# Cosine attention and a hardswish layer: transfers of values by head on 128 partitions, casts in three pieces, biases as immediates

## The chip, the core and the metric

The kernel runs on one core of a Trainium2 chip. The metric is device time in microseconds (us) of one execution; lower is better. Besides TensorE (PE), VectorE (DVE), ScalarE (ACT) and GpSimd (POOL), the core has SyncE (SP), which here only issues DMA transfers, and 16 DMA engines that carry them out.

## What is computed

q, k and v have 8 batches, 12 heads, 448 tokens and 64 elements, in fp32. Attention is on normalised q and k, and its result goes through two matrix products with a hardswish between them (d_model 768, d_ff 2048, 3584 tokens):

```python
q_n = q / (norm(q) + 1e-06);  k_n = k / (norm(k) + 1e-06)
attn = softmax(q_n @ k_n.T / tau)            # tau = 0.1
x = (attn @ v) with the heads side by side   # 3584 x 768
h = x @ w_in
out = (h * clip(h + 3.0, 0.0, 6.0) / 6.0) @ w_out
```

## The kernel before, in words

**Work units.** A *pair* i (0 to 47) is two heads of one batch, A = head n and B = head n + 6, so that a batch is six pairs. Two pairs with neighbouring heads share their transfers: the load d = i // 2 of values brings heads n and n + 1 of group 0 (A) and group 1 (B).

**Tokens.** Token 7p + c of a head is row p (0 to 63) and piece c (0 to 6). Keys and values of one head stand on 128 partitions: rows with pieces 0 to 2 on partitions 0 to 63 and pieces 4 to 6 on partitions 64 to 127. That is three full 128-token groups. Piece 3 of A (partitions 0 to 63) and of B (64 to 127) make up a shared middle group, M.

**Loading values.** `load_v` (L200 to L209) issues four transfers on SP's queue, one for each group g and each half of the partitions: two heads on 64 partitions, four pieces of 64 elements each, 1,024 bytes in a row. One of three buffers of `big` takes them (`vr`, `NV` = 3); each head has five slots of 64 elements there. The lower half fills slots 1 to 4, the upper half slots 0 to 3. The slot that holds no values and yet is cast (4 above for A, 0 below for B) is set to zero once at the start (L968, L969).

**Casting values.** `vcast` (L280 to L288) turns the eight groups of a pair into bf16 in `vx` (four buffers), each with 65 columns, of which the last is 1 for the sum of the softmax. A single instruction on 128 partitions x 512 elements does it, on DVE (as a reduction over one element) for pairs 0 to 3 and on POOL for the others.

**Using values.** `values` (L457 and around) multiplies the exponentials by `vx` on PE into PV. For the middle group it takes all 128 rows for pairs below `FIRST` = 18, where the other head's half of `vx` must be zero; from pair 18 on it takes only the 64 rows that belong to the head.

**The order of work.** Every engine runs its instructions in the order in which they are written. Up to pair 17 that order is written out by hand in `PLAN`, with short names (`LQ` load q or k, `LV` load_v, `SQ` and `RE` squares and their sums, `NO` norms, `NM` normalise, `VC` vcast, `XD` transpose q and k by DMA, `CK`, `CS` and `CQ` copies of the transposed k and q, `SC` scores, `EX` exponentials, `VA` values, `FI` finish, `U` a unit of the layer). From pair 18 on, a loop writes one iteration for each pair; `VC` of pair i + 2 stands in iteration i, `XD` of the next two pairs in every even one, `LQ` of i + 7 in each and `LV` of load (i + 5) // 2 in every odd one. SP's queue holds the loads of q and k (L197), of values (L209), the transposes by DMA (L325, L509, L521) and most stores of the result (L603), all in that order. The weights come by POOL's queue. `busy_pv` (L923) and `busy` (L918) put matmuls on zeros in between at the start.

**Biases.** `norms` (L256) adds 1e-6 and `relu` in `mm1_unit` (L577) adds 0.5 through `bias=` from a tile of two columns, which two memsets fill (L972, L973). `relu` writes `u`, and DVE multiplies it into `gT` (L583).

Of the kernel before, what the change touches and what calls it, by code (L numbers as in the profile page):

```python
# [8 lines left out]
FP32 = mybir.dt.float32  # L9
BF16 = mybir.dt.bfloat16  # L10
AF = mybir.ActivationFunctionType
ALU = mybir.AluOpType
AX = mybir.AxisListType

EPS = 1e-6


FIRST = 18
# [43 lines left out]
def kernel(  # L62
# [10 lines left out]
    nc = tc.nc  # L73
    B, H, S, D = q.shape
# [3 lines left out]
    HP = H // 2  # L78
# [12 lines left out]
    const = ctx.enter_context(tc.tile_pool(name="const", bufs=1))  # L91
# [12 lines left out]
    KC = FCN // 2  # L104
# [13 lines left out]
    NV, NR = 3, 7  # L118


    RAW, VAL, SUM = 14 * D, 20 * D, KC * 128 // 2
    big = const.tile([128, (NR + 2) * RAW + NV * VAL], FP32, name="big", tag="big")

    def item(n):
        return big[:, n * RAW : (n + 1) * RAW].rearrange("p (g c d) -> p g c d", g=2, c=7)

    vr = [
        big[:, c : c + VAL].rearrange("p (i c d) -> p i c d", i=4, c=5)
        for c in range((NR + 2) * RAW, (NR + 2) * RAW + NV * VAL, VAL)
    ]  # L130
    NVX = 4
    vx = [const.tile([128, 8, D + 1], BF16, name=f"vx{i}", tag=f"vx{i}") for i in range(NVX)]
# [13 lines left out]
        [const.tile([128, 2, 14], FP32, name=f"{x}{i}", tag=f"{x}{i}") for x in ("ln", "nr", "le", "r")]  # L146
        for i in range(2)
    ]
    bias = const.tile([128, 2], FP32, name="bias", tag="bias")
    eps_bias, half_bias = bias[:, 0:1], bias[:, 1:2]  # L150
    ident = const.tile([128, 128], BF16, name="ident", tag="ident")

    PV = psum.tile([128, 2, 512], FP32, name="PV", tag="PV")
# [10 lines left out]
    engines = {"v": nc.vector, "p": nc.gpsimd, "a": nc.scalar, "s": nc.sync}  # L164
    issued = set()

    def needs(*what):
        for w in what:
            assert w in issued or any(x < 0 for x in w[1:] if isinstance(x, int)), w
# [31 lines left out]
    def load_v(d):  # L201
        needs(("VC", 2 * (d - NV)), ("VC", 2 * (d - NV) + 1))
        b, n = 2 * d // HP, 2 * d % HP
        for g in range(2):
            f = v[b, HP * g + n : HP * g + n + 2].rearrange("i (p c) d -> p i (c d)", c=7)
            t = vr[d % NV][:, 2 * g : 2 * g + 2, :, :].rearrange("p i c d -> p i (c d)")
            for half in range(2):
                o = t[64 * half : 64 * half + 64, :, (1 - half) * D : (5 - half) * D]
                nc.sync.dma_start(out=o, in_=f[:, :, 3 * half * D : (3 * half + 4) * D])  # L209

    def square(j, e, c0, n):

# [33 lines left out]
    def norms(d, *items):  # L246

        needs(("NM", 2 * d - 4), ("NM", 2 * d - 3))
        items = items or (0, 1)
        for x in items:  # L250
            needs(("RE", 2 * d + x))
        it = slice(items[0], items[-1] + 1)
        ln, nr, le, r = (t[:, it, :] for t in rs[d % 2])
        nc.scalar.activation(out=ln, in_=n2s[d % 2][:, it, :], func=AF.Ln)
        nc.scalar.activation(out=nr, in_=ln, func=AF.Exp, scale=0.5)
        nc.scalar.activation(out=le, in_=nr, func=AF.Ln, bias=eps_bias)  # L256
        nc.scalar.activation(out=r, in_=le, func=AF.Exp, scale=-1.0)  # L257
        for x in items:
            issued.add(("NO", d, x))
# [19 lines left out]

    def vcast(i, e):  # L280
        needs(("LV", i // 2), ("VA", i - NVX, 3))
        t = vr[i // 2 % NV][:, i % 2, 1:5, :]
        f = bass.AP(tensor=t.tensor, offset=t.offset, ap=[t.ap[0], [9 * D, 2], [D, 4], [1, D]])
        o = vx[i % NVX][:, :, 0:D].rearrange("p (g c) d -> p g c d", g=2)
        if e == "v":
            nc.vector.tensor_reduce(out=o, in_=f.rearrange("p g c (d x) -> p g c d x", x=1), axis=AX.X, op=ALU.max)
            return
        (engines[e].copy if e == "a" else engines[e].tensor_copy)(out=o, in_=f)  # L288

    z_of = {}  # L290
    unread = {}
# [1 line left out]
    def bank_of(name, reads):  # L293

        bank = {"Y": Y, "Z": Z}[name] if name else next_bank()
        key = id(bank)
        assert not unread.get(key), name
        unread[key] = reads
        return bank, key
# [231 lines left out]

    def tail(c, n):

        assert 2 * RAW <= c and c + n <= (NR + 2) * RAW + NV * VAL
        return big[:, c : c + n]

    TAIL = 2 * RAW
    g_last = tail(TAIL, FCN * (S + SR) // 2).bitcast(BF16).rearrange("p (f n) -> p f n", f=FCN)
    TAIL += FCN * (S + SR) // 2

    def g_of(b):
        if b == B - 1:
            needs(("NM", NP - 1), ("RE", NP - 1), ("VC", NP - 1))
            return g_last
        return gT[b % 2]
# [16 lines left out]
    def mm1_unit(b, fc):  # L562
        needs(*(("CX", i) for i in range(b * HP, (b + 1) * HP)))
        assert len(weights) <= 6 - 2 * (2 * fc // FCN)
        x, g, c0 = xT[b % 2], g_of(b), b % 2 * SR
        ps, key = bank_of(None, 1)
        for cc in range(CC):
            nc.tensor.matmul(  # L568
                ps[:, 0:S],
                w_in_sb[:, cc, fc * 128 : (fc + 1) * 128],  # L570
                x[:, cc, 0:S],
                start=(cc == 0),
                stop=(cc == CC - 1),
            )
        def relu():
            u = sb.tile([128, S], BF16, name="u", tag="u", bufs=3)
            nc.scalar.activation(  # L577
                out=u[:, :], in_=ps[:, 0:S], func=AF.Relu, bias=half_bias, scale=1.0 / 6.0
            )
            post["v"].append(lambda: product(u))  # L580

        def product(u):
            nc.vector.scalar_tensor_tensor(  # L583
                out=g[:, fc, c0 : c0 + S],
                in0=u[:, :],
                scalar=1.0,
                in1=ps[:, 0:S],
                op0=ALU.min,
                op1=ALU.mult,
            )  # L590
            unread[key] = 0
            g_done.add((b, fc))

        post["a"].append(relu)

    def result(b, t, cols, o, end=None):
# [39 lines left out]
    def firsts(b, *fcs):  # L636
        return [(mm1_unit, b, fc) for fc in fcs]

    def second(b):
# [12 lines left out]
    banks, parts, ready = {}, {}, set()  # L652
    late_sums = [
        {x: tail(c, SUM).bitcast(BF16).rearrange("p (c n) -> p c n", c=KC) for x, c in zip("167e", range(c, c + 4 * SUM, SUM))}
        for c in (TAIL, TAIL + 3 * SUM)
    ]
    late_sums[0].pop("e")
    TAIL += 7 * SUM
    wide = [big[:, c : c + MH] for c in range(0, 3 * MH, MH)]
    wide_late = [tail(c, MH) for c in range(TAIL, TAIL + 2 * (len(PAIRS) - LOOP) * MH, MH)]  # L660

    def sum_of(n, what):
# [211 lines left out]
    for b in range(2, B - 1):  # L874
        first = firsts(b, *range(FCN))
        for n, x in enumerate([0, 3, 3, 3, 3, 2]):
            i = (b + 1) * HP + n
            u = carry + [first.pop(0) for _ in range(x)]
            carry = []
            *p, last = products(TURNS[i])  # L880
            if i == NP - 1:
                p, last = [last], None
            x = 0 if n == 1 else 1 if n in (0, 5) and i > FIRST else 2
# [5 lines left out]
    b = B - 1  # L889
    f = firsts(b, *range(FCN))  # L890
# [50 lines left out]
    def whole_units(n, engines="av"):  # L941
# [5 lines left out]

    OPS = {
        "LQ": load_qk, "LV": load_v, "W": next_weights, "SQ": square, "RE": reduce, "NO": norms,
        "NM": normalise, "VC": vcast, "TR": transposes, "XD": crossbar, "XB": back_crossbar, "XP": back_two, "CQ": copy_q, "CK": copy_k, "CS": copy_k3, "SC": scores,  # L950
        "EX": exps, "VA": values, "FI": finish_values, "BK": back, "CX": copy_x, "U": unit, "UA": lambda: finish_units("a"), "UV": lambda: finish_units("v"),
        "GL": g_left, "WS": lambda x, *h: weight_sums(str(x), *((h[0] * KC // 2, KC // 2) if h else (0, KC))), "UU": whole_units, "D": busy, "DP": busy_pv, "OPEN": open_ring,
# [11 lines left out]
            do(op, *(int(a) if a.lstrip("-").isdigit() else a for a in args))  # L964


    for t in vr:
        nc.vector.memset(t[64:128, 0:2, 4, :], 0.0)  # L968
        nc.vector.memset(t[0:64, 2:4, 0, :], 0.0)  # L969
    zeros = xT[1][:, 0, :]  # L970
    nc.vector.memset(zeros, 0.0)
    nc.vector.memset(eps_bias, EPS)  # L972
    nc.vector.memset(half_bias, 0.5)  # L973
    make_identity(nc, ident)
    for t in vx:
        nc.vector.memset(t[:, :, D : D + 1], 1.0)
        nc.vector.memset(t[64:128, 3, D : D + 1], 0.0)
        nc.vector.memset(t[0:64, 4, D : D + 1], 0.0)
    for t in kz:
        nc.gpsimd.memset(t[:, :], 0.0)  # L980
    nc.gpsimd.memset(km[:, :, :], 0.0)
# [18 lines left out]
    for i in range(FIRST, NP):  # L1000
# [36 lines left out]
        n = 2  # L1037
# [59 lines left out]
```

## Time and profile before

| | |
|---|---|
| median of 3 runs | 405.61 us (405.17 to 407.64) |
| the profiled execution, its span | 405.6 us |
| busy: PE, DVE, ACT, POOL | 396.2, 288.9, 278.3, 233.5 us |
| granted clock of PE, mean | 0.998 |
| mean over DMA | 161 GB/s |
| values transfers to landing: shortest, median, longest | 2.6, 4.9, 11.1 us |

A span goes from the first to the last instruction of one execution. A line of a group names the line of the program, the engine, the operation, what is written and read, the shape and the count; then the busy time in us and the mean of one in ns; and last the idle time of the engine just before, with what ended it. A line of the stretches gives the stretch, its length, the busy time of each engine with the number of instructions, the granted clock of PE, the share of the 16 DMA engines' time in which they worked and the rate. A line of the queues gives packets, MB and the share of 16 engines; a line of the issues gives the count, the size of one and the median from issue to landing.

### The profile page before, as it was taken

The numbers are of one execution on the slowest core, as the hardware profiler recorded it, in microseconds if no ns is written. First come the engines' busy times: TensorE is split into PE (matmuls) and PEld (weight loads), VectorE is DVE, ScalarE is ACT, GpSimd is POOL, SyncE is SP. The second block draws the span as 40 slices with busy tenths as digits, with TensorE's granted clock in tenths as the row PEclk, the third lists the DMA queues.
The fourth block names the chain that finished last, engine by engine and source line by source line (L and its number), as shares of the span: only waits on it lengthen the run. The fifth ranks groups of instructions, "written<-read, shape, count | busy, mean of one in ns | idle before, by whom it ended". The sixth has DMA issues, their size and how long they took to land.

```text
span 405.6 us, 9619 instructions
## 1 busy us (share of the span) xinstructions
PE 396.2 (98%) x3696; PEld 234.5 (58%) x3696; DVE 288.9 (71%) x503; ACT 278.3 (69%) x609; POOL 233.5 (58%) x228
## 2 busy tenths in 40 slices
PE   7899999999989999999999999999999999999996
PEld 4666565555655555655555556556555556555554
DVE  5888777766998777777857887587656666645663
ACT  4899998888467687687767778778757755225230
POOL 6799645761483996587475874886674600410060
PEclk9999999999999999999999999999999999999999
DMA  8899989979988749886799649977964522140134
GB/s 286 251 251 244 236 237 226 184 112 192 223 208 190 184 109 199 200 220 143 172 196 223 132 129 180 184 194 144 188 158 86 112 45 58 40 87 20 24 75 99
DMA packets 91566, 65.32 MB, mean 161 GB/s; under 512 B 56064, under 2 KB 89984, under 8 KB 91520
## 3 DMA queue, kind: packets, MB, share of 16 engines
q1 hardware_dynamic: 87408, 58.02, 62.4%
q0 software_dynamic: 3712, 6.29, 9.0%
q8 instruction: 29, 0.48, 0.5%
q10 hardware_dynamic: 400, 0.39, 0.3%
q14 instruction: 17, 0.14, 0.1%
HBM read 47.19 MB, written 11.01 MB: 143 GB/s over the span
## 4 chain that ended last, share of the span: by engine, by line
PE 91%; DVE 3%; DMA 3%; POOL 1%; SPq 1%; issue 0%; DVEq 0%; POOLq 0%
PE M L568 24%; PE M L741 17%; PE PV L457 13%; PE Y L568 6%; PE M L417 6%; PE Z L568 5%; PE Y L741 4%; PE Z L741 3%; PE M L615 3%; DMA big<-in_q_dram 3%; PE M L821 2%; PE Z L417 2%; PE Z L821 1%; PE Y L417 1%; PE PV L923 1%; PE SC L417 1%
## 5 line engine op out<-in xcount | busy, mean ns | idle before, releaser
L435 ACT ACTIVATE at<-M 128x448 bf16<-128x448 f32 x200 | 99.8, 567 | 16.4 <-PE M L417 14.3
L568 PE MATMUL M<-xT,w_in_sb 128*128 128x448 bf16 x522 | 110.7, 352 | 0.0
L568 PEld LDWEIGHTS <-w_in_sb 128*128 128x128 bf16 x768 | 71.9, 98 | 62.4 <-issue 2.5
L269 POOL TENSOR_TENSOR nrm<-big,r 128x896 bf16<-128x896 f32 (+1 forms) x48 | 79.4, 1658 | 26.0 <-ACT r L257 19.2
L577 ACT ACTIVATE u<-M,bias 128x448 bf16<-128x448 f32 x87 | 57.0, 655 | 26.0 <-PE M L568 25.5
L583 DVE SCALAR_TENSOR_TENSOR gT<-u,M 128x448 bf16<-128x448 bf16 x76 | 46.8, 618 | 38.0 <-ACT u L577 37.3
L226 POOL TENSOR_TENSOR big<-big 128x896 f32<-128x896 f32 (+3 forms) x39 | 63.4, 1628 | 10.0 <-DVE rc L477 5.1
L457 PEld LDWEIGHTS <-at 128*128 128x128 bf16 (+1 forms) x1536 | 54.8, 97 | 24.0 <-issue 14.7
L457 PE MATMUL PV<-vx,at 128*128 128x65 bf16 (+1 forms) x1536 | 64.3, 194 | 0.2 <-DVE on L478 0.2
L238 DVE TENSOR_REDUCE n<-big 128x14 f32<-128x896 f32 (+1 forms) x50 | 51.9, 1041 | 6.2 <-ACT big L224 5.5
L374 POOL COPY km<-tT 64x128 bf16<-64x128 bf16 x34 | 12.7, 372 | 59.6 <-DMA tT<-nrm 44.1
L770 POOL TENSOR_TENSOR big<-big 128x384 f32<-128x384 f32 x11 | 11.8, 1071 | 54.7 <-ACT big L789 54.6
L741 PEld LDWEIGHTS <-gT 128*128 128x128 bf16 x288 | 27.8, 98 | 20.5 <-DVE gT L719 0.8
L741 PE MATMUL M<-w_out_sb,gT 128*128 128x384 bf16 x208 | 37.9, 326 | 0.3 <-DVE gT L719 0.3
L288 POOL CAST vx<-big 128x512 bf16<-128x512 f32 x44 | 33.5, 765 | 3.5 <-DMA big<-in_v_dram 2.4
L435 ACT ACTIVATE at<-Z 128x448 bf16<-128x448 f32 x49 | 27.7, 565 | 9.9 <-PE M L417 7.1
L478 DVE TENSOR_TENSOR on<-PV,rc 128x512 bf16<-128x512 f32 x48 | 33.2, 691 | 1.7
L417 PE MATMUL M<-tT,kz 64*128 64x448 bf16 (+1 forms) x175 | 31.9, 351 | 1.0 <-DVE o L628 1.0
L741 PEld LDWEIGHTS <-gs 128*128 128x128 bf16 x224 | 21.6, 98 | 14.5
L568 PE MATMUL Y<-xT,w_in_sb 128*128 128x448 bf16 x132 | 28.6, 353 | 0.0
L435 ACT ACTIVATE at<-Y 128x448 bf16<-128x448 f32 x45 | 25.7, 570 | 3.1 <-PE Z L417 2.9
L741 PE MATMUL M<-w_sum,gs 128*128 128x384 bf16 x144 | 26.3, 326 | 0.0
(133 smaller groups left out, 565.2 us busy)
## 6 DMA issues: line engine op xcount, KB each, us to landing
big<-in_v_dram SPq DMA_DIRECT2D x96, 128.0 KB, 4.9
big<-in_k_dram SPq DMA_DIRECT2D x24, 448.0 KB, 5.3
big<-in_q_dram SPq DMA_DIRECT2D x24, 448.0 KB, 4.3
out_dram<-o SPq DMA_DIRECT2D x107, 96.0 KB, 2.2
w_in_sb<-in_moe_w_in_dram POOLq DMA_DIRECT2D x4, 768.0 KB, 10.2
w_out_sb<-in_moe_w_out_dram POOLq DMA_DIRECT2D x4, 768.0 KB, 9.1
tT<-nrm SPq DMA_TRANSPOSE x34, 3.4
xT<-on SPq DMA_TRANSPOSE x25, 3.8
```

Of the source, the lines that this page charges most:

```text
L226: engines[e].tensor_tensor(out=o, in0=i, in1=i, op=ALU.mult)
L238: nc.vector.tensor_reduce(out=n2s[d % 2][:, j % 2, c], in_=sq[:, :, :, :].rearrange("p g c d -> p (g c) d")[:, c, :], axis=AX.X, op=ALU.add,)
L269: engines[e].tensor_tensor(out=nrm[:, :, g, :].rearrange("p c g d -> p g c d"), in0=raw_of[j][:, g, :, :], in1=rs[d % 2][3][:, j % 2, :] . ...
L288: (engines[e].copy if e == "a" else engines[e].tensor_copy)(out=o, in_=f)
L417: nc.tensor.matmul(o, ks, qt[rows], start=True, stop=True)
L435: nc.scalar.activation(out=o, in_=x, func=AF.Exp, scale=inv_tau)
L457: nc.tensor.matmul(pv_out(j, h), at[rows, n, q_cols(i // HP, j)], vt[rows, 3 + h if name == "M" else 5 * h + int(name[1]), :], start=(name ...
L478: nc.vector.tensor_tensor(out=on[:, :, :, :].rearrange("p j h d -> p h j d"), in0=pv4[:, :, :, 0:D], in1=rc[:, :, :].to_broadcast([128, 2, ...
L568: nc.tensor.matmul(ps[:, 0:S], w_in_sb[:, cc, fc * 128 : (fc + 1) * 128], x[:, cc, 0:S], start=(cc == 0), stop=(cc == CC - 1),)
L577: nc.scalar.activation(out=u[:, :], in_=ps[:, 0:S], func=AF.Relu, bias=half_bias, scale=1.0 / 6.0)
L583: nc.vector.scalar_tensor_tensor(out=g[:, fc, c0 : c0 + S], in0=u[:, :], scalar=1.0, in1=ps[:, 0:S], op0=ALU.min, op1=ALU.mult,)
L741: nc.tensor.matmul(m, lhs[:, c, :], rhs[:, c, c0 : c0 + width], start=(base is None and c == 0), stop=(c == KC - 1), skip_group_check=True,)
```

## The change

- `load_v` issues four transfers again, each with one head on 128 partitions, four pieces (1,024 bytes) in a row. The source pattern has a count of 2 for the halves of the partitions, outermost, put ahead of the 64 rows. Group 0 takes pieces 0 to 3 and 4 to 7, group 1 pieces -1 to 2 and 3 to 6; piece 7 and piece -1 are those of the neighbouring row.
- The buffers have four slots a head in place of five. `big` keeps its size.
- The slot that was zero now holds those neighbours' values. For pairs 0 to 17 `vcast` therefore casts in three pieces: 128 x 384, 64 x 64 and 64 x 64. From pair 18 on it is one piece of 128 x 512, with the neighbours' values in the halves that `values` does not read.
- The zeros of `vx` are set over 65 columns in place of one; the memsets of `vr` go.
- The biases 1e-6 and 0.5 are immediates; their tile and its two memsets go.

```diff
-    RAW, VAL, SUM = 14 * D, 20 * D, KC * 128 // 2
-    big = const.tile([128, (NR + 2) * RAW + NV * VAL], FP32, name="big", tag="big")
+    RAW, VAL, SUM = 14 * D, 16 * D, KC * 128 // 2
+    BIG = (NR + 2) * RAW + NV * 20 * D
+    big = const.tile([128, BIG], FP32, name="big", tag="big")
...
-        for g in range(2):
-            f = v[b, HP * g + n : HP * g + n + 2].rearrange("i (p c) d -> p i (c d)", c=7)
-            t = vr[d % NV][:, 2 * g : 2 * g + 2, :, :].rearrange("p i c d -> p i (c d)")
-            for half in range(2):
-                o = t[64 * half : 64 * half + 64, :, (1 - half) * D : (5 - half) * D]
-                nc.sync.dma_start(out=o, in_=f[:, :, 3 * half * D : (3 * half + 4) * D])
+        for h in range(4):
+            f = v[b, HP * (h // 2) + n + h % 2].rearrange("(p c) d -> p (c d)", c=7)[:, 0 : 4 * D]
+            f = bass.AP(tensor=f.tensor, offset=f.offset - h // 2 * D, ap=[[4 * D, 2]] + list(f.ap))
+            o = vr[d % NV][:, h, :, :].rearrange("p c d -> p (c d)")
+            nc.sync.dma_start(out=o, in_=f)
...
-        nc.scalar.activation(out=le, in_=nr, func=AF.Ln, bias=eps_bias)
+        nc.scalar.activation(out=le, in_=nr, func=AF.Ln, bias=EPS)
...
-        t = vr[i // 2 % NV][:, i % 2, 1:5, :]
-        f = bass.AP(tensor=t.tensor, offset=t.offset, ap=[t.ap[0], [9 * D, 2], [D, 4], [1, D]])
-        o = vx[i % NVX][:, :, 0:D].rearrange("p (g c) d -> p g c d", g=2)
-        if e == "v":
-            nc.vector.tensor_reduce(out=o, in_=f.rearrange("p g c (d x) -> p g c d x", x=1), axis=AX.X, op=ALU.max)
-            return
-        (engines[e].copy if e == "a" else engines[e].tensor_copy)(out=o, in_=f)
+        t, o = vr[i // 2 % NV], vx[i % NVX]
+
+        def part(p, x, n, w):
+            s, c = 2 * (x // 4) + i % 2, x % 4
+            f = t[p, s : s + 1, c, :]
+            f = bass.AP(tensor=f.tensor, offset=f.offset, ap=[f.ap[0], [(12 - n) * D, w], [D, n], [1, D]])
+            y = o[p, x : x + 1, 0:D]
+            y = bass.AP(tensor=y.tensor, offset=y.offset, ap=[y.ap[0], [(8 - n) * (D + 1), w], [D + 1, n], [1, D]])
+            return f, y
+
+        if i < FIRST:
+            parts = [part(slice(0, 128), 0, 3, 2), part(slice(0, 64), 3, 1, 1), part(slice(64, 128), 4, 1, 1)]
+        else:
+            parts = [part(slice(0, 128), 0, 4, 2)]
+        for f, y in parts:
+            if e == "v":
+                nc.vector.tensor_reduce(out=y, in_=f.rearrange("p g c (d x) -> p g c d x", x=1), axis=AX.X, op=ALU.max)
+            else:
+                (engines[e].copy if e == "a" else engines[e].tensor_copy)(out=y, in_=f)
...
-                out=u[:, :], in_=ps[:, 0:S], func=AF.Relu, bias=half_bias, scale=1.0 / 6.0
+                out=u[:, :], in_=ps[:, 0:S], func=AF.Relu, bias=0.5, scale=1.0 / 6.0
...
-    for t in vr:
-        nc.vector.memset(t[64:128, 0:2, 4, :], 0.0)
-        nc.vector.memset(t[0:64, 2:4, 0, :], 0.0)
...
-    nc.vector.memset(eps_bias, EPS)
-    nc.vector.memset(half_bias, 0.5)
...
-        nc.vector.memset(t[64:128, 3, D : D + 1], 0.0)
-        nc.vector.memset(t[0:64, 4, D : D + 1], 0.0)
+        nc.vector.memset(t[64:128, 3, :], 0.0)
+        nc.vector.memset(t[0:64, 4, :], 0.0)
```

## The prediction

> **What bounds the kernel now.** I read the page first: busy time, queues, the chain, the DMA issues.
>
> ```profile
> span 405.6 us, 9619 instructions
> ...
> PE 396.2 (98%) x3696; PEld 234.5 (58%) x3696; DVE 288.9 (71%) x503; ACT 278.3 (69%) x609; POOL 233.5 (58%) x228
> ...
> q1 hardware_dynamic: 87408, 58.02, 62.4%
> q0 software_dynamic: 3712, 6.29, 9.0%
> ...
> PE 91%; DVE 3%; DMA 3%; POOL 1%; SPq 1%; issue 0%; DVEq 0%; POOLq 0%
> ...
> big<-in_v_dram SPq DMA_DIRECT2D x96, 128.0 KB, 4.9
> big<-in_k_dram SPq DMA_DIRECT2D x24, 448.0 KB, 5.3
> ```
>
> PE is busy 98% of the span and is 91% of the chain, so an edit on another engine gains little. Only 9.4 us of the span are without PE. The second thing to see is the DMA load: 62.4 + 9.0 = 71.4% of 16 engines, or 290 us on each engine if it is spread evenly. That is second only to PE and holds only while it is spread.
>
> Then I read the stretches, cut at the issue of the last values transfers (301.3 us) and at the last values cast (323.9 us):
>
> ```profile
> core 0: us, PE busy (x) PEld busy (x) DVE busy (x) ACT busy (x) POOL busy (x), PEclk, DMA share, GB/s
> 5.00:10.00 5.00, 5.00 (x23) 2.65 (x22) 2.82 (x6) 2.68 (x8) 2.66 (x3) 1.00 1.04 373
> 0.00:301.30 301.30, 295.82 (x2939) 175.73 (x2940) 230.03 (x407) 232.18 (x517) 208.24 (x202) 1.00 0.87 193
> 301.30:323.90 22.60, 22.60 (x217) 13.22 (x215) 13.32 (x23) 16.20 (x37) 11.22 (x15) 1.00 0.53 112
> 323.90:405.60 81.70, 77.81 (x544) 45.55 (x542) 45.58 (x74) 29.96 (x57) 14.09 (x13) 0.99 0.25 56
> ```
>
> While values are being loaded the 16 engines are 87% busy, so none of them has room for much more. The first line gives the rate of one engine under load: 373 GB/s over 16 engines at a share of 1.04 is 22.4 GB/s, or 45.7 ns for 1,024 bytes.
>
> The timeline of SP's queue shows the pace of the values loads (start, time for four issues):
>
> ```profile
> 208.94 2.66 SPq L209 DMA_DIRECT2D big<-in_v_dram  x4
> ...
> 299.26 2.66 SPq L209 DMA_DIRECT2D big<-in_v_dram  x4
> ```
>
> There are seven loads from the first to the second line, so a load comes every (299.26 - 208.94)/6 = 15.05 us. Last, the groups with shapes kept apart, for the edits on the engines:
>
> ```profile
> L577 ACT ACTIVATE u<-M,bias 128x448 bf16<-128x448 f32 x87 | 57.0, 655 | 26.0 <-PE M L568 25.5
> L435 ACT ACTIVATE at<-M 128x448 bf16<-128x448 f32 x200 | 99.8, 567 | 16.4 <-PE M L417 14.3 <-PE Y L417 1.7
> L288 POOL CAST vx<-big 128x512 bf16<-128x512 f32 x44 | 33.5, 765 | 3.5 <-DMA big<-in_v_dram 2.4 <-PE Z L314 1.0
> L286 DVE TENSOR_REDUCE vx<-big 128x512 bf16<-128x512 f32 x4 | 2.6, 675 | 0.0
> L374 POOL COPY km<-tT 64x128 bf16<-64x128 bf16 x34 | 12.7, 372 | 59.6 <-DMA tT<-nrm 44.1 <-PE M L417 13.1 <-PE Z L417 1.4
> L336 DVE COPY kz<-Z 64x64 bf16<-64x64 bf16 x16 | 3.0, 186 | 0.1
> ```
>
> **The edits on the engines.** *Biases:* 87 + 22 + 19 = 128 of `u` at 655, 649 and 654 ns, where the exponential of the same shape takes 567: 128 x 0.088 = 11.3 us less on ACT. 25 of `le` at 318 against 243 for `ln`: 1.9 us less. ACT waited 25.5 us for PE just before `u`, so this lengthens a wait. On the path lie only the three `le` of the start: 0.2 us. I take 0; the ends are -0.2 and, if every `u` were waited for, a gain capped by PE's 9.4 us.
>
> *Casts of pairs 0 to 17:* 14 are on POOL, 4 on DVE. A three-quarter piece costs between 3/4 of the whole and the whole: 0.46 to 0.61 us on POOL (median of L288 612 ns), 0.51 to 0.67 on DVE. A 64x64 piece on POOL lies between the 205 ns memset of 128x128 and the 372 ns copy of 64x128, on DVE at the 186 ns copy. So POOL pays 0.87 to 1.36 us for 0.61, about 0.5 more, 7 us in all; DVE 0.88 to 1.04 for 0.67, about 0.25 more, 1.0 in all. Three DVE casts stand at 17.8 to 19.9 us ahead of a copy that PE needs: 0.7 us on the path. POOL is full from 20 to 40 us, where 3 of its casts stand, so up to 1.5 us there; later it idles over a quarter of the time, which hides the rest. Sum of the casts: 0.7, ends 0 and 7.7 (all of POOL's and the three on DVE).
>
> *Memsets:* six of 0.17 us and two of 0.06 go; eight of one column (0.06 us) grow to 65 columns, at most 0.17 each as 64x128 fp32 does. DVE saves 0.2 to 1.1 us before its first data at 4.21 us, for which it had waited 0.72 us: 0. Without that cover it would be a gain of that size.
>
> *Issues on SP:* still 96, at 0.607 us the median. At the 0.46 us of a first q or k issue SP would save 14 us; SP mostly waits for results (38.2 us for DVE at L603), so 0. The cast of a pair now needs two of the four transfers, and a transfer waits for two casts fewer: both earlier or equal, 0.
>
> **The transfer itself decides.** Bytes (131,072), rows (128 of 1,024 bytes) and count are as before; the source pattern is not. Before, both sides began with 64 partitions. Now the destination begins with 128 partitions and the source with a count of 2 (the halves, 4 x 64 elements apart), then 64, then 256 elements. No row shows a transfer whose pattern begins with a count under 64, so I bound its cost from both sides. One end is that it spreads as before: 0. Before, it did spread: the fastest landed in 2.6 us, 50 GB/s with its latency, above two engines' 44.8. The other end is that it is cut along its outermost count, which leaves two shares on two engines:
>
> - Values on each of the two: 96 x 64 = 6,144 rows x 45.7 ns = 281 us. By the mean of q1 (62.4% x 16 x 405.6 us over 58.02 MB = 71.5 ns for 1,024 bytes) 439 us.
> - All else before the last values issue: 0.87 x 301.3 = 262 us on each engine, less the values' old part there, 768 x 71.5 ns = 55: 207 us. If all of its bytes went at 22.4 GB/s: (58.02 + 6.29 - 12.58) MB/16/22.4 = 144 us, 90% of it before 301.3: 130.
> - The start, 3.8 us, and the stretch from the last cast to the end, 81.7 us.
>
> The sum is 3.8 + 281 + 130 + 81.7 = 497 to 3.8 + 281 + 207 + 81.7 = 574; with 439 for the values 732. I take 45.7 ns, from the stretch of back-to-back loads, since it is the row nearest to a queue of 1,024-byte rows. Between 497 and 574 I take 555, nearer the upper: most of the other packets are small (56,064 under 512 bytes) and do not move at 22.4 GB/s. The check by the pace: one load is 256 x 45.7 ns = 11.7 us on each of the two engines, the rest of 15.05 us at the share of 0.87 is 13.1 - 2.3 = 10.8 (2.3 being 32 rows at 71.5), 22.5 in all, 7.4 over the pace; 20 to 24 loads of that are 148 to 178 us: 554 to 583. The engines' edits hide behind this: casts wait for values, and PE waits for casts.
>
> SP's queue and the two engines are shared: behind four values issues stand the transposes of q and k, the q and k loads and the result stores. They land late by up to 11.7 us, and kz (DVE), km (POOL) and the scores (PE) wait for them; that is how the delay reaches PE beside the values themselves.
>
> I choose two engines because the count of 2 is the only dimension along which the source can be cut into whole blocks in the order of its rows. That it was cut this way no row shows. The Trainium skill, "DMA: Bandwidth & Descriptors", section "Why a DMA increments its semaphore by 16 and not by 1", says that the number of engines is the largest up to 16 that divides the slowest dimension above 1 of both sides: of 128 and 2 that is 2. Its table gives some 27 GiB/s for an engine, by which the values would take an estimated 217 us in place of 281, and the sum would be 491. The same page's "Rules for kernel authors" speak for one 128-partition transfer in place of two on partition halves; by that the sum would be that of the first rival.
>
> **Rivals.**
>
> 1. *The transfer spreads over 16 engines.* Then only the edits on the engines count: 405.6 + 0.7 - 0.2 = 406.1. For it: bytes and rows are the same, and the destination counts 128. Against: the outermost count of the source.
> 2. *It spreads, and the three-piece casts reach the path.* POOL, full from 20 to 40 us, delays the normalised q and k that PE transposes: 405.6 + 7.7 = 413.3 at most. It decides over 1% once 4.1 us of it reach PE; against it, POOL idles 42% of the span.
> 3. *It spreads and lands sooner: faster.* The place is the start, where SP waited 4.6 us for k, 4.2 for q and 1.7 for values to land before it issued values. If landings fell from 4.9 to the shortest, 2.6, 47% of these 10.5 us would go, and all behind them would come 4.9 us earlier: 400.7. It decides from 4.1 us on. Against it: 8.8 of the 10.5 us are for q and k, which do not change.
> 4. *Two engines, but hidden by loads three ahead.* 281 + 130 us do not fit into 297 us: no chance.
>
> **The numbers.** Two engines 0.82: 555, own range 480 to 700 (0.97 of it; below 497 if waits overlap better, up towards 732 if packets on two engines run at the mean price). Rival 1 0.11, rival 2 0.04, rival 3 0.03. So 480 to 700 holds 0.82 x 0.97 = 0.80. About 1% is what a measurement of this kernel can tell from no change: faster 0.03, same 0.11, slower 0.86. The sum stands on the profiled execution, whose span is 405.6 us; the median of the runs is 405.61.
>
> **What would show it.** Right: the landing of `big<-in_v_dram` from 4.9 us to 12 or more; PE at some 70%, with casts waiting for values and km and kz for transposes; mean GB/s from 161 to 118. The page named above says that each engine used ends its share with an increment of its own; by that the packets would fall by 96 x 14 from 91,566 to 90,222. Wrong: a landing under 6 us with PE still at 98%; then rivals 1 to 3 are told apart by POOL's wait for casts and the landing in the first 30 us. The engines' steps: `u` at 567 ns, three casts on POOL at some 1.1 us together, SP's issue at 0.46 to 0.61.

## The result and the profile after

| | before | after |
|---|---|---|
| median of the runs | 405.72 us (4 runs) | 573.88 us (4 runs, 572.06 to 577.35) |
| ratio | | 1.414, 95% interval 1.408 to 1.421 |
| profiled execution, span | 405.6 us | 570.3 us |
| granted clock of PE, mean | 0.998 | 0.874 |

The change makes the kernel 168 us slower. The page of the changed kernel, in the lines that answer to those shown of before:

```profile
span 570.3 us, 9656 instructions
...
PE 430.8 (76%) x3696; PEld 246.1 (43%) x3696; DVE 285.6 (50%) x503; ACT 268.9 (47%) x609; POOL 233.4 (41%) x256
...
DMA packets 90222, 65.32 MB, mean 115 GB/s; under 512 B 54720, under 2 KB 88640, under 8 KB 90176
...
q1 hardware_dynamic: 86064, 58.02, 51.5%
...
PE 49%; DMA 23%; SPq 18%; DVE 5%; ACT 2%; issue 2%; POOL 1%; POOLq 0%; DVEq 0%
PE M L578 13%; SPq L207 13%; PE M L751 9%; DMA xT<-on 8%; PE PV L467 7%; DMA big<-in_v_dram 6%; DMA tT<-nrm 5%; DMA big<-in_k_dram 4%; PE Y L578 4%; PE Z L578 3%; PE M L427 3%; PE Y L751 3%; SPq L335 2%; SPq L196 2%; PE Z L751 2%
```

No engine is busy for more than 76%, and the mean over the 16 DMA engines has fallen, not risen: 51.5% of their time on this queue, after 62.4%. Yet DMA and the queue of SP are now 41% of the chain, and the issues of values alone (L207) are 13%, as much as the largest group of matmuls. A mean over 16 engines hides a queue in front of two. The bytes are the same (65.32 MB), and the packets are 1,344 fewer, 14 for each of the 96 values transfers. This is the count that the prediction gave for two engines in place of 16.

The packet records of the trace show the two engines more directly. They name no engine, but a packet of 1,024 bytes is always a row of values, so one can count how many of them are under way at once. In the changed kernel it is exactly two for 78% of the time in which any is under way, and never more than four; before, it was up to 23. All in all, values are under way for 282 us, where it had been 88.

The waits name what came late:

```profile
POOL km L384 <- DMA tT<-nrm: 132.2, 14, 14.8
...
POOL vx L298 <- DMA big<-in_v_dram: 66.5, 10, 12.8
...
PE M L578 <- DMA xT<-on: 38.0, 6, 8.3
...
DVE kz L374 <- DMA tT<-nrm: 34.2, 8, 7.6
```

The casts of values wait, but the transposes, which the change does not touch, are waited for longer. They stand behind the values in SP's queue. That queue shows how they are held up. These are the first values load of the start and most of one turn of the loop:

```profile
3.89 9.19 SPq L207 DMA_DIRECT2D big<-in_v_dram  x4
...
310.43 5.80 SPq L207 DMA_DIRECT2D big<-in_v_dram  x4
316.33 5.24 SPq L531 DMA_TRANSPOSE xT<-on  x1
321.67 3.69 SPq L335 DMA_TRANSPOSE tT<-nrm  x2
325.45 1.19 SPq L613 DMA_DIRECT2D out_dram<-o  x2
326.69 0.58 SPq L196 DMA_DIRECT2D big<-in_q_dram  x1
327.38 1.20 SPq L519 DMA_TRANSPOSE xT<-on  x1
```

The four issues of the first load took 3.38 us before and take 9.19 now; those in the loop mostly took 2.66 and take 5.8 to 7.0. The transpose of `xT` behind them took 1.3 and takes 5.24. The second column is the time for which SP was held by the issue. When it is held can be read in this turn: the first two of the four issues still take 0.60 and 0.55 us, the next two 1.88 and 2.63. The 512 rows of the load are under way from 313.0 to 323.9 us, and from 325.4 us on the issues of stores and loads take about 0.6 us each, as they did before the change. So SP is held while the two engines still have rows of values to move. The view of line L207 sums it up:

```profile
L207 SPq DMA_DIRECT2D big<-in_v_dram x96: 544/2582/11174, 3.9 to 459.9; - x96
```

The median issue is 2.58 us, where it was 0.61. Two engines need 64 x 45.7 ns = 2.9 us for the rows of one transfer. Added up to the last values issue, SP's issues come to 199 us of 302 before and to 426 us of 462 after: SP now issues 92% of that time.

### The profile page after: what moved, and what is told of

It is laid out like the page before. It is cut to its first block, busy times and chain, and to the rows that moved or that the text cites. A ratio compares the mean times of both kernels' runs of the same rounds, so it can differ in the third digit from the quotient of the medians.

```text
span 570.3 us, 9656 instructions
## 1 busy us (share of the span) xinstructions
PE 430.8 (76%) x3696; PEld 246.1 (43%) x3696; DVE 285.6 (50%) x503; ACT 268.9 (47%) x609; POOL 233.4 (41%) x256
## 2 busy tenths in 40 slices
DMA packets 90222, 65.32 MB, mean 115 GB/s; under 512 B 54720, under 2 KB 88640, under 8 KB 90176
## 3 DMA queue, kind: packets, MB, share of 16 engines
q1 hardware_dynamic: 86064, 58.02, 51.5%
## 4 chain that ended last, share of the span: by engine, by line
PE 49%; DMA 23%; SPq 18%; DVE 5%; ACT 2%; issue 2%; POOL 1%; POOLq 0%; DVEq 0%
PE M L578 13%; SPq L207 13%; PE M L751 9%; DMA xT<-on 8%; PE PV L467 7%; DMA big<-in_v_dram 6%; DMA tT<-nrm 5%; DMA big<-in_k_dram 4%; PE Y L578 4%; PE Z L578 3%; PE M L427 3%; PE Y L751 3%; SPq L335 2%; SPq L196 2%; PE Z L751 2%
## 5 line engine op out<-in xcount | busy, mean ns | idle before, releaser
L578 PE MATMUL M<-xT,w_in_sb 128*128 128x448 bf16 x522 | 125.2, 384 | 50.8 <-DMA xT<-on 38.0
L578 PEld LDWEIGHTS <-w_in_sb 128*128 128x128 bf16 x768 | 76.4, 104 | 126.0 <-issue 73.8
L587 ACT ACTIVATE u<-M 128x448 bf16<-128x448 f32 x87 | 48.7, 559 | 92.2 <-PE M L578 90.2
L467 PE MATMUL PV<-vx,at 128*128 128x65 bf16 (+1 forms) x1536 | 69.6, 200 | 18.8 <-POOL vx L298 15.1
L467 PEld LDWEIGHTS <-at 128*128 128x128 bf16 (+1 forms) x1536 | 59.6, 101 | 48.4 <-issue 37.0
L384 POOL COPY km<-tT 64x128 bf16<-64x128 bf16 x34 | 9.9, 290 | 137.3 <-DMA tT<-nrm 132.2
L298 POOL CAST vx<-big 128x512 bf16<-128x512 f32 (+2 forms) x72 | 33.5, 476 | 77.2 <-DMA big<-in_v_dram 66.5
L427 PE MATMUL M<-tT,kz 64*128 64x448 bf16 (+1 forms) x175 | 36.6, 392 | 23.5 <-DMA tT<-nrm 23.0
L427 PEld LDWEIGHTS <-kz 64*128 64x128 bf16 (+1 forms) x296 | 14.3, 97 | 74.4 <-DVE kz L374 32.5
L578 PE MATMUL Y<-xT,w_in_sb 128*128 128x448 bf16 x132 | 32.0, 384 | 0.0
L222 ACT ACTIVATE big<-big 128x896 f32<-128x896 f32 (+4 forms) x12 | 9.0, 768 | 44.4 <-DMA big<-in_k_dram 39.8
```

What stands on the lines that cost most here:

```text
L427: nc.tensor.matmul(o, ks, qt[rows], start=True, stop=True)
L467: nc.tensor.matmul(pv_out(j, h), at[rows, n, q_cols(i // HP, j)], vt[rows, 3 + h if name == "M" else 5 * h + int(name[1]), :], start=(name ...
L578: nc.tensor.matmul(ps[:, 0:S], w_in_sb[:, cc, fc * 128 : (fc + 1) * 128], x[:, cc, 0:S], start=(cc == 0), stop=(cc == CC - 1),)
L587: nc.scalar.activation(out=u[:, :], in_=ps[:, 0:S], func=AF.Relu, bias=0.5, scale=1.0 / 6.0)
```

## The experiments

In each, the time is the median, and the ratio to the kernel before comes from runs on the same chip.

**Only the outermost count: 128, 4, 8.** Everything of the change stays except the source pattern.

```diff
-            f = bass.AP(tensor=f.tensor, offset=f.offset - h // 2 * D, ap=[[4 * D, 2]] + list(f.ap))
+            f = bass.AP(tensor=f.tensor, offset=f.offset - h // 2 * D, ap=[[7 * D // 2, 128], [1, 4 * D]])
```

> The changed kernel with one thing different: the source of a values transfer is one count of 128 rows (a row every 3.5 pieces) in place of 2 x 64. Bytes, rows of 1,024 bytes, destination on 128 partitions, number of transfers, casts and biases stay; the rows hold other values than the reference needs, so only its time counts. Theory A (the transfer is cut along its outermost count, so the changed kernel uses two engines): the time goes back to 406.1 us, within 400 to 413, and the landing of values is under 8 us. Theory B (128 partitions as destination, or reading neighbours' rows, makes the transfer slow): it stays at 560 to 580. Theory C (three-piece casts hold POOL up): it stays at 560 to 580.

Measured: 405.61 us, ratio 1.001 (0.998 to 1.004). Theory B (the 128 partitions or the neighbours' rows make the transfer slow) and theory C (the casts do) fall. The page of this kernel has the packets of before again, and a landing:

```profile
DMA packets 91566, 65.32 MB, mean 161 GB/s; under 512 B 56064, under 2 KB 89984, under 8 KB 91520
...
big<-in_v_dram SPq DMA_DIRECT2D x96, 128.0 KB, 4.0
```

```diff
+            f = bass.AP(tensor=f.tensor, offset=f.offset - h // 2 * D, ap=[[75 * D, 4], [7 * D, 32], [1, 4 * D]])
```

> The changed kernel with the source of a values transfer as 4 x 32 rows in place of 2 x 64; same bytes, rows, destination and count; the rows overlap and hold other values than the reference needs, so only its time counts. Theory A: four engines take 3,072 rows of 45.7 ns each, 140 us in place of 281; with 207 us of other transfers that is 347 us of the 301 us before the last values issue, so the DMA still binds a little: 421 us, within 408 to 440. Theories B and C: 560 to 580.

Measured: 460.81 us, ratio 1.135 (1.130 to 1.141).

```diff
+            f = bass.AP(tensor=f.tensor, offset=f.offset - h // 2 * D, ap=[[48 * D, 8], [7 * D, 16], [1, 4 * D]])
```

> The same with 8 x 16 rows; the values are again not those of the reference. Theory A: eight engines take 1,536 rows each, 70 us; with 207 us of other transfers that is 277 of 301 us, so PE binds again: 406 to 412 us. Theories B and C: 560 to 580.

Measured: 418.73 us, ratio 1.030 (1.026 to 1.034). The time follows the outermost count: 573.9, 460.8, 418.7 and 405.6 us for 2, 4, 8 and 128. The packets follow too. First the page with 4, then the page and the chain with 8:

```profile
DMA packets 90414, 65.32 MB, mean 143 GB/s; under 512 B 54912, under 2 KB 88832, under 8 KB 90368
```

```profile
DMA packets 90799, 65.32 MB, mean 157 GB/s; under 512 B 55297, under 2 KB 89217, under 8 KB 90753
...
PE 68%; DMA 18%; POOL 6%; DVE 3%; issue 2%; SPq 1%; ACT 1%; POOLq 0%
```

That is 1,152 = 96 x 12 fewer than before with 4, and 767, one off 96 x 8, with 8. The rows under way at once say the same: with 4 the most frequent number is 4, with 8 it is 8, and with 128 there are 16 or more for 23% of the time. The theory of the outermost count stands, but both times lie above the ranges that it gave, by 21 us and by 7. The expectation had only set the work on each engine against the time there is. With 4, SP's issues of values come to 106 us, where they are 47 with 128, and the longest single one is 6.4 us, so the queue is held here too. With 8 they come to 66 us and SP is 1% of the chain, so its queue does not set the pace there; transfers are 18% of it, and those of values 11%.

**The rest of the change with the transfers of before.** Four slots, casts in pieces and immediates stay; each transfer takes two heads on 64 partitions.

```diff
-        for h in range(4):
...
+        for g in range(2):
+            t = vr[d % NV][:, 2 * g : 2 * g + 2, :, :].rearrange("p i c d -> p i (c d)")
+            for half in range(2):
+                f = v[b, HP * g + n : HP * g + n + 2].rearrange("i (p c) d -> p i (c d)", c=7)[:, :, 0 : 4 * D]
+                f = bass.AP(tensor=f.tensor, offset=f.offset + (4 * half - g) * D, ap=list(f.ap))
+                nc.sync.dma_start(out=t[64 * half : 64 * half + 64, :, :], in_=f)
```

> The changed kernel with its four slots, casts, memsets and biases, but each values transfer as before the change: two heads on 64 partitions, source and destination both starting with 64; the same bytes go to the same places as in the changed kernel. Theory A: 406.1 us, as the first rival of the prediction has it (0.7 more for casts, 0.2 less for biases), within 403 to 410. Theory C: 560 to 580, since all of the cast work is there. Theory B in its part on neighbours' rows: 560 to 580; in its part on 128 partitions: 406.

Measured: 406.14 us, ratio 1.002 (1.000 to 1.004). This is the same computation as the changed kernel, neighbours' rows included. So the rest of the change costs nothing that can be told, and the loss lies in the shape of the transfer, with all that follows from it.

**The biases alone, the casts alone**, each put into the kernel before.

```diff
-        nc.scalar.activation(out=le, in_=nr, func=AF.Ln, bias=eps_bias)
+        nc.scalar.activation(out=le, in_=nr, func=AF.Ln, bias=EPS)
...
-                out=u[:, :], in_=ps[:, 0:S], func=AF.Relu, bias=half_bias, scale=1.0 / 6.0
+                out=u[:, :], in_=ps[:, 0:S], func=AF.Relu, bias=0.5, scale=1.0 / 6.0
```

> The kernel before with only the biases as immediates (no tile of biases, no memsets of it). The prediction's step: u from 655 to 567 ns, 11.3 us less busy time on ACT, and no change of the time beyond 0.2 us less: 405.4, ratio 0.999 to 1.000. The rival, that ACT's time is on PE's path through u and gT: up to 9.4 us less, 396 to 401.

Measured: 405.17 us, ratio 1.000 (0.998 to 1.002). ACT is busy for 266.1 us in place of 278.3, 12.2 us less, and no change of the time can be told.

```diff
+        if i < FIRST:
+            parts = [part(slice(0, 128), 0, 3, 2), part(slice(0, 64), 3, 1, 1), part(slice(64, 128), 4, 1, 1)]
```

> The kernel before with only the casts of pairs 0 to 17 in three pieces (and the zeros of vx over 65 columns); transfers and biases as before. The prediction's step: POOL 7 us busier, DVE 1.0, of which 0.7 us reach the end: 406.3, ratio 1.001 to 1.003. The rival, that POOL, full from 20 to 40 us, hands on most of it: up to 413.

Measured: 405.96 us, ratio 1.001 (0.999 to 1.003). The groups of this kernel:

```profile
L300 POOL CAST vx<-big 64x64 bf16<-64x64 f32 x28 | 8.1, 288 | 0.8
L300 POOL CAST vx<-big 128x384 bf16<-128x384 f32 x14 | 7.1, 505 | 2.3 <-DMA big<-in_v_dram 2.1
L298 DVE TENSOR_REDUCE vx<-big 128x384 bf16<-128x384 f32 x4 | 2.2, 552 | 0.1
L298 DVE TENSOR_REDUCE vx<-big 64x64 bf16<-64x64 f32 x8 | 1.7, 210 | 0.1
```

Three pieces cost POOL 0.505 + 2 x 0.288 = 1.08 us and DVE 0.552 + 2 x 0.210 = 0.97 us.

**More lead.** Each load of the loop is issued two pairs earlier in the changed kernel.

```diff
+    do("LV", 12)
...
-            prepare(("LV", (i + 5) // 2))
+            prepare(("LV", (i + 7) // 2))
```

> The changed kernel with each load of values in the loop issued two pairs earlier, which is as soon as its buffer is cast; all else as changed. Theory A1 (the two engines are full until the last values have landed, so the sum of their work sets the time): the lead changes nothing, 565 to 585. Theory A2 (each load only comes too late for its cast, there being too little lead): the waits for values go and the time falls below 540.

Measured: 574.35 us, ratio 1.417 (1.413 to 1.421). Lead changes nothing, so A2 (too little lead) falls. The last row of values is through 11.7 us earlier than in the changed kernel (458.4 after 470.1 us), and yet the last cast starts at 488.7 us after 488.5.

**Another queue for the values: ACT, POOL.**

```diff
-            nc.sync.dma_start(out=o, in_=f)
+            nc.scalar.dma_start(out=o, in_=f)
```

> The changed kernel with the values transfers issued from ACT in place of SP, in the same places of the order of work; two engines as changed. Theory A1 (the sum of the work on the two engines sets the time): the same work stands on the same two engines, 560 to 585. Theory A3 (SP's queue, which takes a median of 2.6 us to issue a values transfer in place of 0.6 and holds up the transposes behind it, sets the time): the transposes come sooner and the time falls to 480 to 540, with km waiting far less than 132 us for tT.

Measured: 595.54 us, ratio 1.469 (1.464 to 1.474), above both ranges. SP is free (173 us of issues in 483 us), and km waits 43.7 us for tT in place of 132.2, as A3 (SP's queue sets the time) had it. But now ACT is held: its issues of values take 186 us, and its waits show what stands behind them:

```profile
ACT at L445 <- DMA big<-in_v_dram: 83.0, 11, 15.8
ACT at L445 <- issue: 46.2, 5, 13.0
```

The exponentials stand behind the issues of values. A3 is not refuted by this, since the hold moved to an engine that has to compute as well.

```diff
-            nc.sync.dma_start(out=o, in_=f)
+            nc.gpsimd.dma_start(out=o, in_=f)
```

> The changed kernel with the values transfers issued from POOL in place of SP, in the same places of the order of work; source patterns as changed. POOL pays some 0.76 us for each issue, by the weights' issues (793 and 736 ns), 73 us in all, on 233 busy. Theory A in its strict form (a transfer with an outermost count of 2 always goes to the same two engines, on any queue): 560 to 600. Theory A in its weaker form (it goes to two engines, but from POOL not always to the same; the Trainium skill, "DMA: Bandwidth & Descriptors", section "Why a DMA increments its semaphore by 16 and not by 1", says that there they follow a cursor that goes round): the load is spread in the mean, and the time falls below 450, with POOL the engine that is late.

Measured: 491.93 us, ratio 1.214 (1.210 to 1.219): 82 us of the loss come back, which is between the two forms of the theory. An issue holds POOL for 0.82 us and no longer:

```profile
L207 POOL DMA_DIRECT2D big<-in_v_dram x96: 789/822/952, 8.7 to 383.7; - x96
```

The transposes still land late, with a median of 8.0 us against 3.4 before. The packet records settle one of the two forms. Values go in packets of 4,096 bytes here, and five or more of them are under way for 28% of the time in which any is, up to 12 at once, where the changed kernel has never more than four. So the transfers did not all go to the same two engines, and the strict form falls. The time under 450 us of the weaker form (two engines, but not always the same) did not come either: km still waits 72.1 us for tT, and why it does no run here shows.

**What of the other transfers counts: their work or their issues.** The stores before the last values transfers are left out of the changed kernel, then of the kernel before, and then made small.

```diff
     def result(b, t, cols, o, end=None):
+        if ("LV", NP // 2 - 1) not in issued:
+            return
```

> The changed kernel without the stores of results that are issued before the last values transfers: 64 of 114 issues are left out, so those parts of the output are not written. All compute stays. Theory A1 (the sum of the work on the two engines sets the time): a store of 96 KB is 4 rows of 1,536 bytes on each engine, some 104 ns each, so 64 x 4 x 0.104 = 26.6 us less on each of the two: 545, within 530 to 555. Theory A4 (the pace is set by single transfers in turn, values, then transposes, then compute, and not by the sum): under 8 us less.

Measured: 532.17 us, ratio 1.313 (1.310 to 1.317): 41.7 us less than the change, more than the 26.6 of A1 (the work on the two engines sets the time) and near what SP takes to issue them: 64 x 0.58 = 37 us, or 45 us as they add up in the changed kernel. A4 (single transfers in turn set the pace), with under 8 us, falls.

> The kernel before without the same 64 stores; those parts of the output are not written. PE bounds it and its stores are hidden, so both theories expect 402 to 406 us. It is the control for the changed kernel without stores.

Measured: 405.31 us, ratio 1.001 (0.999 to 1.003). In the kernel before the stores cost nothing that can be told.

```diff
     def result(b, t, cols, o, end=None):
+        if ("LV", NP // 2 - 1) not in issued:
+            cols = slice(cols.start, cols.start + 32)
```

> The changed kernel with the same 64 stores issued, but each of 32 columns (8 KB) in place of 384 (96 KB); those parts of the output are written in part only. Without these stores the time fell by 41.7 us, where 26.6 had been worked out from their rows. Theory A5 (the loss of the stores' work on the two engines brought it): the issues stay and the work goes, so the time falls by 20 to 40 us as without them, 535 to 553. Theory A6 (SP's own time to issue them, 64 x 0.58 = 37 us, brought it): the issues stay, so the time stays at 565 to 575.

Measured: 569.8 us, ratio 1.406 (1.401 to 1.412): 4 us less than the change. In the packet records a row of such a store takes 14.0 ns on average, where one of 1,536 bytes takes 103.9, so 64 x 4 x 0.090 = 23 us of work left each engine. Nearly none of it came back as time. A5 (the loss of their work brought the time) falls, and so does A1 in its plain form: the bytes of the other transfers on the two engines are not what fills the time. A6 (SP's time to issue them) stands: the pace is that of SP's queue, which spends 92% of the time issuing.

## Why the prediction was right, and where it was not

**Two engines.** Right. The range 480 to 700 holds 573.9; 555 was 19 us too low. The time follows the dose (2, 4, 8 and 128), and so do the count of packets and the rows under way at once. The Trainium skill's rule in "DMA: Bandwidth & Descriptors", section "Why a DMA increments its semaphore by 16 and not by 1", agrees with all four points. The Trainium skill's rule for one 128-partition transfer (same page, "Rules for kernel authors"), by which the sum would have been that of the first rival, came true here only with an outermost count of 128 in the source.

**The price of a row.** 45.7 ns were taken; the packet records have 47.7 on average, with 65.5 before, when up to 23 rows were under way at once. The term of 281 us came out: values are under way for 282. The bound of 71.5 was far off.

**All else on the engines, 130 to 207 us.** This is the step that failed in its mechanism, though the time came out. It was meant as work of the two engines beside the values. Between the first row of values (9.6 us) and the last (470.1 us) there are 178 us in which none is under way, so the number lay in the range. But the run with tiny stores took some 23 us of that work away and gave back 4 us of time. What adds up is SP's time: 218 us for issues of values (62 before), 68 for transposes of `xT` (25), 57 for those of q and k (42), 45 for stores (39) and 38 for loads of q and k (30), 426 in all, with 36 us in which it did not issue. The prediction saw that transposes, loads and stores stand behind the values, but not that an issue itself is held. It had put SP's issues at nothing. That 130 to 207 held the measured number was luck.

**The stretch behind the last cast.** The last cast starts at 488.5 us, so 81.8 us follow, where 81.7 had been taken over from before; the clock there is 1.00 after 0.99. But the sum went straight from the last values to the last cast, and left out the stretch between them, 22.6 us from the last issue in the prediction's own rows. Here 18.4 us lie between the last row of values and the last cast. The full account of the span is 9.6 + 282.4 + 178.1 + 18.4 + 81.8 = 570.3 us. That the end waits for the last values is not shown: with more lead they came 11.7 us earlier, and the end did not move.

**The pace.** A load every 22.5 us was worked out. The issues of values at 288.00 and, eight loads on, at 456.56 us give 21.1.

**Engines.** `u` takes 559 ns after 655 (567 predicted), `le` 226 after 318. A cast in three pieces costs POOL 0.47 us more than the median of one, 0.612 (0.5 predicted), and DVE 0.30 more (0.25 predicted). POOL is 4.5 us busier, not 7, in the kernel with the casts alone, because the whole casts before had a mean of 0.765, from which three pieces are 0.32 more, or 4.4 us for 14. SP's issue at 128 partitions has a median of 0.43 us, a little under the lower bound of 0.46; that shows only with 128 as the outermost count. All of them together are 406.14, where the first rival had 406.1; a difference of 0.5 us from before is within the interval, so this does not confirm it.

**Rivals.** The first fell with the time itself, and its reason with the rows under way. The second is refuted by the casts alone (1.001), the third by the count of 128: values landed in 4.0 us in place of 4.9, and the time did not move.

**Signs.** The landing of values could not be read as foretold, since the page of the changed kernel gives none; the time of an issue took its place. PE is busy for 76% and not 70%, for its matmuls got longer: at L578 into M a mean of 384 ns after 352, at a granted clock of 0.874, and PE is busy for 34.6 us more in all. Where PE waits for transfers that need not cost anything; how much of the 168 us it did cost was not tried and stays open.

**Open.** What between SP and the two engines fills up and so holds an issue, which no trace here names; whether a store left out saves the time of its issue alone or also what each transfer costs besides its bytes; what set the time with the values on POOL's queue; and what the lower clock of PE cost.

## What to carry to other kernels

Before you reshape a transfer, read the outermost count of both patterns, and not only the bytes, the rows or the partitions. Here that of the source was varied: 96 transfers of the same rows cost nothing with 128, 13 us with 8, 55 us with 4 and 168 us with 2. From SP and ACT, a transfer that is dealt to few engines held the queue that issued it, and much of the loss showed at innocent transfers behind it; from POOL an issue took 0.82 us throughout. When the mean load of the DMA engines falls while waits for transfers grow, look at how long each issue takes.

## What was not expected of the hardware

An issue on SP is not of a fixed length: the same instruction took a median of 0.43 us with an outermost count of 128 on both sides, 0.61 with 64 on both sides and 2.58 with 2 in the source, up to 11.2. The Trainium skill, "DMA: Bandwidth & Descriptors", section "Issuing engines are not separate DMA queues", calls the time to initiate a DMA usually small against the DMA itself. Here SP spent 426 of 462 us on it, and moving the issues of values to ACT cost 22 us more.
